# The head of a two-layer attention and gated-MLP kernel: VectorE's order written out, three of four low halves on GpSimd, filling products, two weights loaded earlier

## The chip, the cores and the metric

One Trainium2 chip, one core. The metric is the device time of one execution in microseconds (us); the times stand beside a profiled execution, whose trace gives every instruction's start and length. Engines: PE (TensorE; its weight loads are listed as PEld), DVE (VectorE), ACT (ScalarE), POOL (GpSimd), and SP (SyncE), whose queue issues all DMAs of this kernel.

## What is computed

x has 2048 rows of 640, in float32. Two blocks, A and B, run twice, one after the other (layer 1 is the first A and B, layer 2 the second):

```python
def A(x, wq, wk, wv, wo, beta):        # x is layer-normed; 32 heads of 20; 4 segments of 512 rows
    for s in range(4):
        logits = q[s] @ k[s].T * 20 ** -0.5 + mask      # inside the segment
        a_dot  = softmax(logits) @ v[s]
        a_mem  = (phi(q[s]) @ M) / (phi(q[s]) @ z + 1e-6)
        out[s] = g * a_mem + (1 - g) * a_dot            # g = sigmoid(beta)
        M, z   = M + phi(k[s]).T @ v[s], z + phi(k[s]).sum(0)
    return out @ wo                    # phi(t) = t + 1 if t > 0 else exp(t)
def B(x, w_in, w_sp, b_sp, w_out):     # x is layer-normed
    z1, z2 = split(gelu(x @ w_in), 2)
    return (z1 * (w_sp @ layernorm(z2) + b_sp)) @ w_out
for _ in range(2):
    x = x + A(layernorm(x)); x = x + B(layernorm(x))
```

## The kernel before

Every large product is done in float16 pairs. An operand is scaled by a power of two, its high half is the value cast to float16, its low half what is left over, and a product is three: high by high, high by low, low by high. For a weight that means, on the way in: a DMA brings it in float32 (five tiles of 128 rows, k = 0 to 4); VectorE takes the largest magnitude of each tile (`tensor_reduce`, `largest`); PE turns the 128 partial maxima into a row, VectorE takes their maximum (`pow2_max`, "turn", tiles `wtp`, `wmx`, `wdg`); PE spreads it over the partitions again and VectorE makes the power of two and its inverse (`pow2_spread`, tiles `wbc`, `pw`, `iv`); then for each k ScalarE writes the high half and VectorE the low half (`split_scaled`, lines L90 and L91).

The program is written as a sequence of Python calls. PE's order is exactly the order of these calls (`manual_schedule`). The other engines and the SP queue are put in order by a planner, which picks by priority and by its own estimate of times; `tc.high_priority` raises the priority of what is issued in it, and `tc.issue_after(i)` keeps what is in it behind instruction i. Each engine then works strictly in its order.

`Attention.head` runs once, ahead of layer 1's attention. It loads the first four tiles of x (512 rows, segment 0), w_q and w_k, and later w_v into staging tiles `wstq`, `wstk`, `wstv` (pool `wpro`); normalises x (`xs`), casts the high halves (`hl`, ScalarE), subtracts the low halves (L1277, two on VectorE, two on GpSimd), and transposes both by four DMAs (L1280) into `xt[0]`. Then come w_q, w_k and w_v, each by maxima, scale, split; between them two units of q (`units("q", 0)`, `units("q", 1)`: 15 products of 512 columns each, into the PSUM tile `qp`), two units of k (`kp`), and at the end four tiles of values (`value(t)`, 30 products of 320 columns each, into `vps`, two PSUM buffers). A unit's output casts it to halves (tile `hl`, two buffers shared by q, k and phi(k)), stores these to DRAM (`st`, L1567 and L1568) and for k also makes phi(k) (L1474, L1476, L1485, L1486) and transposes it by DMA (L1493). `start()` writes constant rows into the tiles that q and k are fetched into.

After the head, `run` goes through steps t = -12, ..., -1 (the lead) and 0, 1, 2, ... Each step can hold score products for the row maxima (`mp`, reduced by VectorE in L1641, from t = -8), score products for the softmax (`es`, from t = 0, exponentiated by ScalarE into `P` in L1631, cast in L1649, low half on GpSimd in L1650), products with values (`pv`), and a share of dense products: further units of q and k, value tiles and output projections, in the order "02 03 v4 04 v5 ...". Streams of side work are given times in steps: `fills` (x tiles for later value tiles: L1356 loads, L303 statistics, L318 and L319 halves, L320 transposes), `background`, `weights`, `reads` and `turned`. In layer 1 the stream `weights` brings w_o from t = -11.9 and the second half of w_in (`wi[1]`, "i1") from t = -9.6, as float32 straight into the tiles where their halves will stand (`Weight.inside`: L120 loads, L123 maxima on VectorE, then a split through a staging tile: L139 and L141 on ScalarE, L142 on GpSimd). Those tiles lie in the pools `topi` and `topo`, on the side of SBUF where the head's staging pool `wpro` lay: w_in's tile over the end of `wstk` and over `wstv`, w_o's over the end of `wstq` and over `wstk`. A tile may be written only when those that lay there before are done with.

Of the kernel before, what the change touches and what calls it, by code (L numbers as in the profile page):

```python
# [9 lines left out]
F32 = mybir.dt.float32  # L10
# [24 lines left out]
HP = 2000  # L35
# [18 lines left out]
def pow2_max(g, pool, psum, tag, am, c0, n):  # L54
# [7 lines left out]
    nc.vector.tensor_scalar(dg[:n, :n], g.ident[:n, :n], mx[:n], None, ALU.mult)  # L62
# [31 lines left out]
class Weight:  # L94
# [17 lines left out]
    def inside(self, stage, psum, t0, pace):  # L112
# [22 lines left out]
        def split(k):  # L135
# [4 lines left out]
            for x, a in zip(full, cs):  # L140
# [986 lines left out]
class Attention:  # L1127
# [96 lines left out]
    def head(self):  # L1224
# [3 lines left out]
        with ExitStack() as ctx:  # L1228
            p = ctx.enter_context(tc.tile_pool(name="wpro", bufs=1, side="right", reuse_waits="tile"))
            ctx.enter_context(tc.high_priority(offset=HP))  # L1230
# [6 lines left out]
            st = {nm: p.tile([128, KD, D], F32, name="wst" + nm) for nm in "qkv"}  # L1237

# [4 lines left out]
            def largest(nm, behind):  # L1243
                a = p.tile([128, KD], F32, tag="wamk" + nm, name="wamk")
                with tc.issue_after(behind):
                    for k in range(KD):
                        nc.vector.tensor_reduce(a[:, k:k + 1], st[nm][:, k], AX.X, ALU.max, apply_absolute_value=True)
                i = WNAMES.index(nm)
                return nc.vector.tensor_reduce(g.wam[:, i:i + 1], a, AX.X, ALU.max).ins

            def scale(nm):
                return pow2_scales(g, self.pl1, self.pm, "ms", g.wam, WNAMES.index(nm), 1)

            def split(nm):
                h, l = g.w[nm]
                return [split_scaled(g, h[:, k], l[:, k], st[nm][:, k], WNAMES.index(nm)) for k in range(KD)]

            def units(nm, m, ps):
                for _ in self.unit(0, m, {nm: ps[:, m]}):
                    pass  # L1260
# [15 lines left out]
            for t in (2, 0, 3, 1):  # L1276
                (nc.gpsimd if t > 1 else nc.vector).tensor_tensor(hl[t][:, 1], xs[t], hl[t][:, 0], ALU.subtract)  # L1277
            for t in (0, 1, 2, 3):
# [15 lines left out]
            with tc.issue_after(i[-1]):  # L1294
                attn_scalars(g)
# [695 lines left out]
```

## Time and profile before

| | us |
|---|---|
| median of 3 runs | 2196.34 (2195.93 to 2196.82) |
| the profiled execution's own time | 2197.64 |
| its span, first to last instruction | 2195.9 |
| first q product of the head | at 24.60 |
| first and last product of the head's value tiles | at 53.12 and 71.1 |
| first softmax tile cast (step 0) | at 121.55 |

| stretch (us) | what runs | PE busy | DVE busy | ACT busy | POOL busy | granted clock |
|---|---|---|---|---|---|---|
| 0 to 53.1 | head up to w_v's split | 21.76 | 43.45 | 19.01 | 14.34 | 0.90 |
| 53.1 to 71.3 | value tiles 0 to 3 | 16.82 | 7.35 | 8.45 | 2.81 | 1.00 |
| 71.3 to 121.5 | the lead | 38.66 | 37.05 | 26.57 | 20.40 | 0.90 |

A row of the timeline gives start and length in us, engine, line of the kernel, operation, output<-inputs, partitions x elements and type, and how many like instructions were merged (x5); in square brackets, how long the engine sat idle before it and what ended that. A row of a table by groups gives total busy time, mean ns of one, idle time before them.

### The profile page before, as it was taken

Reading aid. Unit: us, or ns where it says so; the run is one execution under the profiler, and the core shown is the slowest. Engines: PE = TensorE matmul, PEld = TensorE weight load, DVE = VectorE, ACT = ScalarE, POOL = GpSimd, SP = SyncE. Lnnn points to the kernel's source line nnn. Section 1 sums busy time; section 2 is a strip of 40 time slices with the busy share of each in tenths; the row PEclk is TensorE's granted clock in tenths of the full one; section 3 lists DMA queues with packets and bytes.
Section 4 is the critical chain, followed back from the end, with each engine's and each line's share of the span. In section 5 each row is a group of like instructions: output and inputs, shape, how many; then the busy total and the mean of one; then the engine's idle time right before and its main releaser. Section 6 shows DMA issues by size and latency. Waiting matters only on the chain.

```text
span 2195.9 us, 48888 instructions
## 1 busy us (share of the span) xinstructions
PE 2067.9 (94%) x19725; PEld 1250.9 (57%) x19725; DVE 1625.9 (74%) x2951; ACT 1217.8 (55%) x1490; POOL 1086.5 (49%) x704
## 2 busy tenths in 40 slices
PE   4889899999899998999999999999989999999999
PEld 1455565666555554555555556565665555555555
DVE  8678888787777878999745887787776676565464
ACT  3499888787634443323323998888874244322221
POOL 2298988887523442444320987787873233000000
PEclk9999999999999999999999999999999999999999
DMA  5626635457765967888676244344566353978884
GB/s 165 185 68 202 164 87 143 112 135 155 173 193 145 251 176 221 222 224 251 169 231 146 78 123 111 100 124 115 151 172 145 99 156 111 272 199 207 229 205 115
DMA packets 516499, 358.38 MB, mean 163 GB/s; under 512 B 410160, under 2 KB 452720, under 8 KB 511152
## 3 DMA queue, kind: packets, MB, share of 16 engines
q1 hardware_dynamic: 516272, 355.26, 60.6%
q8 instruction: 154, 2.52, 0.5%
q14 instruction: 73, 0.60, 0.1%
HBM read 159.65 MB, written 107.43 MB: 122 GB/s over the span
## 4 chain that ended last, share of the span: by engine, by line
PE 66%; DVE 11%; ACT 8%; DMA 5%; issue 5%; POOL 4%; SPq 1%; ACTq 0%; DVEq 0%; POOLq 0%
PE zp L395 13%; PE cyp L595 4%; PE cyp L870 4%; PE ga L547 3%; PE gb L547 3%; PE yps L1421 3%; PE pv L1684 3%; PE b L799 3%; PE a L799 3%; PE qps L1445 3%; ACT P L1631 3%; PE vps L1389 3%; PE mp L1624 3%; PE kps L1445 2%; POOL PHL L1650 2%
## 5 line engine op out<-in xcount | busy, mean ns | idle before, releaser
L1650 POOL TENSOR_TENSOR PHL<-P,PHL 128x1024 f16<-128x1024 f32 x310 | 659.3, 2135 | 179.8 <-ACT PHL L1649 133.0
L1631 ACT ACTIVATE P<-es,sc 128x1024 f32<-128x1024 f32 x320 | 356.0, 1113 | 89.1 <-PE es L1595 84.7
L1641 DVE TENSOR_REDUCE mx<-mp 128x2 f32<-128x1024 f32 (+2 forms) x384 | 320.9, 861 | 82.6 <-PE mp L1595 79.6
L1649 ACT CAST PHL<-P 128x1024 f16<-128x1024 f32 x320 | 333.4, 1042 | 6.3
L395 PEld LDWEIGHTS <-th 128*128 128x128 f16 x1920 | 187.8, 98 | 167.2 <-issue 6.0
L799 PEld LDWEIGHTS <-wt 128*128 128x128 f16 x1344 | 132.1, 99 | 122.8 <-ACT wt L790 6.0
L1684 PEld LDWEIGHTS <-PHL 128*128 128x128 f16 x5120 | 166.8, 96 | 58.7 <-DVE oat L1705 20.6
L306 POOL TENSOR_TENSOR lnrs<-lnve,mhalf 128x1 f32<-128x1 f32 x78 | 49.7, 644 | 301.0 <-DVE lnve L305 247.3
L547 PEld LDWEIGHTS <-wt 128*128 128x128 f16 x1344 | 131.5, 98 | 112.6
L1684 PE MATMUL pv<-vs,PHL 128*128 128x41 f16 x5120 | 172.6, 181 | 21.3 <-DVE oat L1705 16.9
L395 PE MATMUL zp<-w,th 128*128 128x432 f16 x960 | 180.4, 346 | 5.0 <-ACT z L408 5.0
L395 PE MATMUL zp<-wi,th 128*128 128x432 f16 x960 | 180.4, 346 | 0.2 <-DVE xt L1427 0.2
L1445 PEld LDWEIGHTS <-zb 128*128 128x128 f16 x1200 | 103.0, 99 | 102.8 <-issue 8.5
L784 POOL TENSOR_TENSOR f<-wt 128x1024 f32<-128x1024 f16 x32 | 84.8, 2660 | 127.5 <-DVE wt L793 110.0
L1624 PEld LDWEIGHTS <-qk 64*128 64x128 f16 (+1 forms) x1728 | 65.9, 93 | 129.8 <-issue 98.1
L1624 PE MATMUL mp<-qk 60*128 60x512 f16 (+3 forms) x864 | 107.6, 303 | 18.0 <-DVE mx L1641 12.3
L1421 PE MATMUL yps<-wo,o 128*128 128x320 f16 x720 | 120.4, 304 | 0.0
L1624 PE MATMUL es<-qk 64*128 64x256 f16 (+3 forms) x864 | 105.7, 296 | 12.4 <-ACT P L1631 10.1
L870 PE MATMUL cyp<-w,ut 128*128 128x320 f16 (+1 forms) x630 | 88.1, 299 | 0.0
L1638 DVE TENSOR_REDUCE mx<-mp 128x4 f32<-128x1024 f32 x64 | 77.8, 1215 | 11.0 <-PE mp L1595 10.9
L1389 PE MATMUL vps<-zb,w 128*128 128x320 f16 x480 | 81.1, 299 | 4.1 <-DVE phl L1486 4.1
L1595 PE MATMUL es<-big,maskk 64*128 64x128 f16 (+1 forms) x1280 | 82.4, 206 | 1.5 <-issue 1.5
(318 smaller groups left out, 4166.3 us busy)
## 6 DMA issues: line engine op xcount, KB each, us to landing
wr<-in_B_w_sp_dram SPq DMA_DIRECT2D x32, 1024.0 KB
qk<-st SPq DMA_DIRECT2D x216, 120.0 KB
z<-z SPq DMA_DIRECT2D x32, 432.0 KB
cz<-z SPq DMA_DIRECT2D x32, 432.0 KB
turned<-wt SPq DMA_DIRECT2D x24, 512.0 KB
wt<-turned SPq DMA_DIRECT2D x24, 512.0 KB
st<-qhl SPq DMA_DIRECT2D x40, 256.0 KB
st<-khl SPq DMA_DIRECT2D x40, 256.0 KB
```

Of the source, the lines that this page charges most:

```text
L395: nc.tensor.matmul(zp[:, n, :FHH], a[:, k, :], b[:, k, c:c + FHH], start=(k == 0 and j == 0), stop=(k == KD - 1 and j == 2))
L547: nc.tensor.matmul(o[:, :FHH], wt[:, x, m, :], zb[b][:, y, m, :], start=start and i == j == 0, stop=i == NP - 1 and j == 2, skip_group_che ...
L799: nc.tensor.matmul(o[:, :FHH], w[:, x, m, :], zb[b][:, y, m, :], start=start and i == j == 0, stop=i == NP - 1 and j == 2, skip_group_chec ...
L870: nc.tensor.matmul(yp[n][:, :320], a[:kn[k], k, :], b[:kn[k], k, n * 320:(n + 1) * 320], start=(k == 0 and j == 0), stop=(k == KO - 1 and ...
L1421: nc.tensor.matmul(ps, a[:, k, :], b[:, k, c], start=(i == 0), stop=(i == 14))
L1445: nc.tensor.matmul(ps, a[:, k, c], b[:, k, :], start=(i == 0), stop=(i == 14))
L1624: nc.tensor.matmul(out[:, h, o:o + w], a[r, ac], b[r, bc], start=o == 0, stop=False, skip_group_check=True)
L1631: self.last_of["ACT"] = nc.scalar.activation(self.Pf[t], es, AF.Exp, scale=g.esc).ins
L1641: self.last_of["DVE"] = nc.vector.tensor_reduce(mx[:, e, :, i], mp[:, :, o:o + w], AX.X, ALU.max).ins
L1649: nc.scalar.copy(hl[:, 0], P)
L1650: (nc.gpsimd if t < self.T - self.TAIL or t % 2 == 0 else nc.vector).tensor_tensor(hl[:, 1], P, hl[:, 0], ALU.subtract)
L1684: nc.tensor.matmul(pv[:, i, h, 0:PVC - 1], self.P[u][:, x, h, o:o + 128], v[:, j, h0 + h, :], start=first and h == x == 0 and (u, o, i, j) ...
```

## The change

Five things, all in layer 1's head and lead:

- The low half of x tile 0 is made by VectorE directly behind the four normalisations, those of tiles 1 to 3 by GpSimd; the transposes go in the order 0, 1, 2, 3 as before.
- VectorE's order is written out by `issue_after`: w_q's maxima, its scale with two of w_k's maxima in it, w_q's split whole, the other three of w_k's maxima; then w_k's scale and split with w_v's maxima in the same way. `attn_scalars` (13 small VectorE instructions) go behind w_v's scale. The outputs of the two k units are issued behind w_v's split.
- PE gets filling products (`keep_busy`, 128 x 192, into a PSUM tile `idle` that nobody reads): 100 before w_q's turn, 5 and 16 around its spread, 16 behind w_k's spread, 10 behind w_v's.
- Value tile 0 takes its products in another order, both halves of the columns side by side, with w_v's low half last, and is issued before VectorE's low halves of w_v are done.
- w_in's second half and w_o are loaded from the head, behind the closing of `wpro`, and w_in's maxima are issued behind value tile 1. The lead keeps turn and spread of both, w_o's maxima and both splits, w_in before w_o.

```diff
-    def inside(self, stage, psum, t0, pace):
+    def inside(self, stage, psum):
...
-        by = lambda t, pace, f: [(t + pace * k, lambda k=k: f(k)) for k in range(self.nk)]
-        return (by(t0, pace, load) + by(t0 + 1.7, pace, largest) + by(t0 + 5.9, pace * self.cols / D, split),
-                [(t0 + 4.5, turn), (t0 + 5.5, spread)])
+        return load, largest, turn, spread, split
...
+            idle = self.po.tile([128, 512], F32, tag="pv", name="idle")
...
-            def largest(nm, behind):
+            def largest(nm, ks, behind):
                 with tc.issue_after(behind):
-                    for k in range(KD):
+                    for k in ks:
...
-            def split(nm):
+            def split(nm, behind):
                 h, l = g.w[nm]
-                return [split_scaled(...) for k in range(KD)]
+                with tc.issue_after(behind):
+                    return [split_scaled(...) for k in range(KD)]
+            def keep_busy(n, a):
+                for _ in range(n):
+                    nc.tensor.matmul(idle[:, :192], a[:, :128], a[:, :192], start=True, stop=True)
...
-            for t in (2, 0, 3, 1):
-                (nc.gpsimd if t > 1 else nc.vector).tensor_tensor(hl[t][:, 1], xs[t], hl[t][:, 0], ALU.subtract)
+            with tc.issue_after(i.ins):
+                low = nc.vector.tensor_tensor(hl[0][:, 1], xs[0], hl[0][:, 0], ALU.subtract).ins
+            for t in (1, 2, 3):
+                nc.gpsimd.tensor_tensor(hl[t][:, 1], xs[t], hl[t][:, 0], ALU.subtract)
...
-            largest("q", i.ins)
-            scale("q")
-            i = split("q")
-            largest("k", i[1])
-            units("q", 0, qp)
-            scale("k")
-            units("q", 1, qp)
-            i = split("k")
-            largest("v", i[1])
-            with tc.issue_after(i[-1]):
-                attn_scalars(g)
-            units("k", 0, kp)
-            scale("v")
-            units("k", 1, kp)
-            split("v")
-            for t in range(4):
-                for _ in self.value(t):
-                    pass
-                if t == 0:
-                    with self.hold():
-                        self.start()
+            keep_busy(100, g.mask["q"])
+            largest("q", range(KD), low)
+            dg = turn("q")
+            largest("k", (0,), g.seen)
+            keep_busy(5, g.mask["q"])
+            i = largest("k", (1,), spread("q", dg))
+            keep_busy(16, g.mask["q"])
+            i = split("q", i)
+            largest("k", range(2, KD), i[-1])
+            us = [unit("q", 0, qp), unit("q", 1, qp)]
+            run(us[0])
+            run(us[1], 9)
+            dg = turn("k")
+            largest("v", (0,), g.seen)
+            run(us[1])
+            i = largest("v", (1,), spread("k", dg))
+            keep_busy(16, g.mask["q"])
+            i = split("k", i)
+            i = largest("v", range(2, KD), i[-1])
+            us = [unit("k", 0, kp), unit("k", 1, kp)]
+            run(us[0], 15)
+            run(us[1], 9)
+            with tc.issue_after(i):
+                dg = turn("v")
+            run(us[1], 6)
+            i = spread("v", dg)
+            keep_busy(10, g.mask["q"])
+            with tc.issue_after(i):
+                attn_scalars(g)
+            i = split("v", i)
+            ctx.close()
+            g.top = self.tops()
+            self.ws = self.pool("aws", 3)
+            nc.vector.memset(g.wap, 0.0)
+            self.made = {}
+            for w, pool in ((g.wi[1], g.top[1]), (g.wo, g.top[0])):
+                w.whole(pool)
+                self.made[w.nm] = w.inside(self.ws, self.pm)
+                for k in range(KD):
+                    self.made[w.nm][0](k)
+            values = [self.value(t, t == 0) for t in range(4)]
+            run(values[0], 12)
+            with tc.issue_after(i[-1]):
+                run(values[0])
+                run(us[0])
+                run(us[1])
+                run(values[1])
+                for k in range(KD):
+                    self.made["i1"][1](k)
+                with self.hold():
+                    self.start()
+                for it in values[2:]:
+                    run(it)
...
+    def value(self, t, late=False):
...
+        if late:
+            pairs = [(k, a, wh) for k in range(KD) for a in (xh, xl)] + [(k, xh, wl) for k in range(KD)]
+        todo = [(n, i) for i in range(15) for n in range(2)] if late else [(n, i) for n in range(2) for i in range(15)]
...
-                for w, at, pace in (g.wo, -LEAD + 0.1, 0.45), (g.wi[1], -LEAD + 2.4, 0.5):
-                    w.whole(g.top[w is not g.wo])
-                    work, turns = w.inside(self.ws, self.pm, at, pace)
-                    todo += work
-                    scales.extend(turns)
+                _, _, turn, spread, split = self.made["i1"]
+                scales.extend([(1.6 - LEAD, turn), (2.8 - LEAD, spread)])
+                todo += by(3.4, 0.95, split)
+                _, largest, turn, spread, split = self.made["o"]
+                scales.extend([(5.2 - LEAD, turn), (6.4 - LEAD, spread)])
+                todo += by(2, 0.6, largest) + by(8.3, 0.7, split)
```

`g.seen` is the last VectorE instruction of the last turn (`wdg`). `run(it, n)` draws n pieces from a generator, or all that are left. `run(values[0], 12)` draws all of tile 0, its outputs among them.

More of the change, by code (lines that the diff above doesn't have):

```diff
@@ L1237, in head @@
             st = {nm: p.tile([128, KD, D], F32, name="wst" + nm) for nm in "qkv"}
+            parts = {nm: p.tile([128, KD], F32, tag="wamk" + nm, name="wamk") for nm in "qkv"}
+            idle = self.po.tile([128, 512], F32, tag="pv", name="idle")
             def load(nm):
@@ L1383, in value @@
         yield 450
-        for n in range(2):
-            ps = self.pd.tile([128, L], F32, tag="dn", name="vps")[:, :320]
-            i = 0
-            for k in range(KD):
-                for a, b in ((xh, wh), (xh, wl), (xl, wh)):
-                    nc.tensor.matmul(ps, a[:, k, c], b[:, k, n * 320:(n + 1) * 320], start=(i == 0), stop=(i == 14))
-                    i += 1
-                    if i % 3 == 0:
-                        yield 3 * 136
+        pairs = [(k, a, b) for k in range(KD) for a, b in ((xh, wh), (xh, wl), (xl, wh))]
+        if late:
+            pairs = [(k, a, wh) for k in range(KD) for a in (xh, xl)] + [(k, xh, wl) for k in range(KD)]
+        banks = [self.pd.tile([128, L], F32, tag="dn", name="vps")[:, :320] for _ in range(2)] if late else [None] * 2
+        todo = [(n, i) for i in range(15) for n in range(2)] if late else [(n, i) for n in range(2) for i in range(15)]
+        for n, i in todo:
+            k, a, b = pairs[i]
+            if i == 0 and not late:
+                banks[n] = self.pd.tile([128, L], F32, tag="dn", name="vps")[:, :320]
+            nc.tensor.matmul(banks[n], a[:, k, c], b[:, k, n * 320:(n + 1) * 320], start=(i == 0), stop=(i == 14))
+            if i % 3 == 2:
+                yield 3 * 136
+            if i < 14:
+                continue
+            ps = banks[n]
             def out(ps=ps.rearrange("p (h d) -> p h d", d=DH), v=self.vs[s % 2][:, t % 4, n * 16:(n + 1) * 16, :]):
@@ L1725, in combine, with tops @@
         self.post(2, out)
+    def tops(self):
+        return [self.top.enter_context(self.tc.tile_pool(name=n, bufs=1, side="right", reuse_waits="tile")) for n in ("topi", "topo")][::-1]
     def run(self, nseg=NSEG):
@@ L1856, in turned @@
                 f()
-        if self.stacked < 0:
-            self.head()
         g = self.g
         first = not g.wo.made
-        self.ws = self.pool("aws", 3) if first else None
-        g.top = [self.top.enter_context(g.tc.tile_pool(name=n, bufs=1, side="right", reuse_waits="tile")) for n in ("topi", "topo")][::-1]
+        if first:
+            with g.tc.high_priority(offset=HP):
+                self.head()
+        else:
+            self.ws = None
+            g.top = self.tops()
         streams = [[next(it), i, it] for i, it in zip((0, 1, 1.5, 2, 3, 4), (fills(), background(), weights(), dense(), reads(), turned()))]
```

31 lines of the change are left out of this document (16 added, 15 removed).

## The prediction

> **What bounds the kernel now.** I read the page first, then the table of busy time by stage, then the timeline of the first 130 us, because the whole change lies there.
>
> ```profile
> span 2195.9 us, 48888 instructions
> PE 2067.9 (94%) x19725; PEld 1250.9 (57%) x19725; DVE 1625.9 (74%) x2951; ACT 1217.8 (55%) x1490; POOL 1086.5 (49%) x704
> ...
> PE   4889899999899998999999999999989999999999
> ```
>
> PE is 94% busy over the span, but the first slice of 55 us shows 4 tenths: the head is where PE waits. The stages (columns: length, then busy us of PE, PEld, DVE, ACT, POOL, granted clock, DMA share, GB/s):
>
> ```profile
> 0.00:53.10 53.10, 21.76 (x75) 9.19 (x76) 43.45 (x113) 19.01 (x28) 14.34 (x34) 0.90 0.56 170
> 53.10:71.30 18.20, 16.82 (x122) 11.73 (x121) 7.35 (x17) 8.45 (x16) 2.81 (x3) 1.00 0.72 230
> 71.30:121.50 50.20, 38.66 (x272) 19.78 (x270) 37.05 (x74) 26.57 (x47) 20.40 (x19) 0.90 0.52 141
> 120.00:220.00 100.00, 89.46 (x1404) 55.90 (x1403) 82.20 (x162) 96.83 (x119) 92.73 (x52) 1.00 0.45 142
> ```
>
> The first row is the head up to the first product of values, with VectorE the busiest (43.45 of 53.10). The second is the four value tiles. The third is the lead, 12 steps before the first softmax tile is cast (121.55); PE is idle there for 11.5 us and VectorE is busy for 37.05. In the fourth, ScalarE (96.83) and GpSimd (92.73) set the rate. Nothing there counts from the program's start, so a lead that ends earlier should move all that follows by as much.
>
> **The change, part by part.** *x's low halves and the q scale.* Today VectorE measures four rows of w_q before it makes two of the low halves:
>
> ```profile
> 11.49 2.18 DVE L1274 TENSOR_SCALAR xs<-xs,mvx,rsx 128x640 f32<-128x640 f32 x4 [1.22 <-POOL rsx L1272]
> 14.19 2.75 POOL L1277 TENSOR_TENSOR xhl<-xs,xhl 128x640 f16<-128x640 f32 x2 [2.73 <-ACT xhl L1275]
> 15.61 6.60 SPq L1280 DMA_TRANSPOSE zb<-xhl  x4
> 16.49 1.12 DVE L1277 TENSOR_TENSOR xhl<-xs,xhl 128x640 f16<-128x640 f32 x1
> 18.27 0.81 DVE L1277 TENSOR_TENSOR xhl<-xs,xhl 128x640 f16<-128x640 f32 x1
> 19.08 0.14 DVE L1249 TENSOR_REDUCE wam<-wamk 128x1 f32<-128x5 f32 x1
> 21.84 3.71 ACT L90 ACTIVATE zb<-wstq,iv 128x640 f16<-128x640 f32 x5 [4.54 <-DVE iv L83]
> 24.60 3.38 PE L1445 MATMUL qp<-zb,zb 128*128 128x512 f16 x8 [3.76 <-DMA zb<-xhl]
> ```
>
> After it, VectorE makes one low half directly behind the last normalisation (it ends at 13.67, 11.49 + 2.18) and POOL three, at 2.75/2 = 1.38 each from about 13.4. They end near 14.8, 14.8, 16.2 and 17.6 instead of 19.08 for the last. Four transposes at 6.60/4 = 1.65 then issue until about 21, and land when the first product can start at 22 to 23. VectorE saves one low half (0.8), so the scale and w_q's split come about 1.0 earlier, at 20.8. First q product: about 22.5 instead of 24.60. The 1.12 against 0.81 of the same instruction is the one that ran while POOL's second one (to 16.94) was still running: the two engines slow each other. The Trainium skill, "GPSIMD Engine Reference", section Specifications, says that GpSimd's SBUF interfaces are shared with VectorE when VectorE reads two SBUF inputs; the trace agrees with 0.3 us, and by that rule VectorE's one low half beside POOL's would cost 1.12. That speaks against the move to GpSimd, but for 0.3 us.
>
> *The order of VectorE: w_k and w_v measured before or behind a split, not in its middle.*
>
> ```profile
> 24.30 3.71 DVE L1247 TENSOR_REDUCE wamk<-wstk 128x1 f32<-128x640 f32 x5
> 27.93 2.46 DVE L91 SCALAR_TENSOR_TENSOR zb<-wstq,iv,zb 128x640 f16<-128x640 f32 x3
> 28.86 1.98 PE L1445 MATMUL qp<-zb,zb 128*128 128x512 f16 x7 [0.89 <-DVE zb L91]
> 32.26 3.40 PE L1445 MATMUL qp<-zb,zb 128*128 128x512 f16 x15 [0.32 <-DVE qhl L1469]
> 35.97 3.71 DVE L1247 TENSOR_REDUCE wamk<-wstv 128x1 f32<-128x640 f32 x5
> 39.60 2.46 DVE L91 SCALAR_TENSOR_TENSOR zb<-wstk,iv,zb 128x640 f16<-128x640 f32 x3
> 40.53 2.69 PE L1445 MATMUL kp<-zb,zb 128*128 128x512 f16 x7 [3.15 <-DVE zb L91]
> ```
>
> Five maxima (3.71) stand in the middle of w_q's split and again in w_k's; PE waits 0.89 and 3.15 for the rest. With the split first: w_q's five low halves run 21.7 to 25.9 (0.84 each, from 2.46/3), the q product ends near 26.5 instead of 30.84. Two of w_k's maxima sit in the scale's idle time, the other three end at 28.2. Turn and spread cost what they cost today (19.08 to 21.84, 2.7), with six q products between; plus 0.7 for a q output on VectorE. w_k's split then starts at about 32 and ends at 37.4; today it ends at 39.60 + 2.46 = 42.06. So minus 4.7.
>
> *w_v and the first value tile.*
>
> ```profile
> 41.99 0.14 DVE L241 TENSOR_SCALAR sc<-pw 128x1 f32<-128x1 f32 x1
> 44.50 0.69 DVE L1469 SCALAR_TENSOR_TENSOR khl<-kp,khl 128x512 f16<-128x512 f32 x1 [0.55 <-ACT eq L1468]
> 48.30 4.99 PE L1445 MATMUL kp<-zb,zb 128*128 128x512 f16 x15 [1.70 <-DVE iv L83]
> 49.20 4.07 DVE L91 SCALAR_TENSOR_TENSOR zb<-wstv,iv,zb 128x640 f16<-128x640 f32 x5 [0.90 <-ACT zb L90]
> 53.12 8.31 PE L1389 MATMUL vps<-zb,zb 128*128 128x320 f16 x60
> 55.85 0.49 DVE L1395 SCALAR_TENSOR_TENSOR vs<-vps,vs 128x320 f16<-128x320 f32 x1
> ```
>
> Now the k outputs (four VectorE instructions of 0.69 and a little more) stand between w_v's maximum and its spread; they go behind w_v's split. Mine: three maxima end at 39.7, scale at 43, 13 small scalars (about 0.13 each, 1.7) among five low halves (4.07), end about 48.7 instead of 53.27, minus 4.6. The low-half products of value tile 0 come last in its order, so its 30 products run while the split does, and it ends at 49.2. Today it ends at 53.12 + 30 x 8.31/60 = 57.3. Minus 8.1. Tiles 1 to 3 need 90 x 0.139 = 12.5. VectorE has more to do in that stretch than it does today: eight value outputs (0.49, 3.9 in all), both k outputs (5.9) and w_in's maxima (row below, 5.0), together 14.8 against 12.5. I add 1.3 for PE waiting for a bank: values end at 63.0 instead of 71.3, **minus 8.3**.
>
> *The filling products.* About 150 products of 192 columns go in front of and between the chains, on an idle PE. At the warm rate (0.227 for 512 columns, 3.40/15) one is 0.085 us, so the 16 are 1.4, less than the VectorE and ScalarE work that they cover (scale, then 0.74 + 0.84 for the first split). If cold they are 2.7 and could delay a split's first product by 1.
>
> ```profile
> 40.00:45.00 5.00, 3.05 (x8) 0.73 (x8) 4.42 (x18) 1.17 (x2) 0.00 (x0) 0.63 0.05 17
> 45.00:50.00 5.00, 2.28 (x7) 1.18 (x8) 4.00 (x14) 2.95 (x5) 0.00 (x0) 0.50 0.45 142
> ```
>
> After the 3.15 us gap the clock falls to 0.63 and 0.50, and products of 512 columns take 0.42. Two stretches of some eight products (from 24.60, 3.38 for 8, and from 48.30) cost 8 x 0.2 = 1.6 each, and five cost 1.0 in the lead (row 89.14 below). Between 0 and 3 us of gain over the first two; they hide partly behind VectorE's pace, so I take 0 beyond the times above. The Trainium skill, "TensorE: Matmul & The Clock Gate", section Why this matters for your kernels, puts the loss at idle gaps above about 3 us: the trace agrees (0.89 cost nothing, 3.15 did). By that rule most fillers cover gaps too short to matter, and only the first hundred change anything.
>
> *w_in and w_o earlier.* Ten loads (5 x 320 + 5 x 432 KB, 3.8 MB) leave the lead's start, and five of VectorE's maxima.
>
> ```profile
> 70.36 5.23 SPq L120 DMA_DIRECT2D wi<-in_B_w_in_dram  x1
> 85.97 0.89 DVE L303 BATCH_NORM_STATS2 lnst<-xt 128x6 f32<-128x320 f32 x2 [4.32 <-DMA xt<-in_A_x_dram]
> 88.56 2.00 DVE L123 TENSOR_REDUCE wap<-wi 128x1 f32<-128x864 f32 x2
> 88.70 0.40 PE L1624 MATMUL mp<-qk 60*128 60x384 f16 x4 [4.18 <-DVE mx L1641]
> 89.14 2.32 PE L1445 MATMUL k<-zb,zb 128*128 128x512 f16 x5
> 95.48 0.58 PE L70 MATMUL wbc<-wdg,ones 1*128 1x1 f32 x2 [4.03 <-DVE wdg L62]
> L123 DVE TENSOR_REDUCE wap<-wi 128x1 f32<-128x864 f32 x5 | 5.0, 1037 | 0.0
> wo<-in_A_wo_dram SPq DMA_DIRECT2D x5, 320.0 KB
> wi<-in_B_w_in_dram SPq DMA_DIRECT2D x5, 432.0 KB
> 121.55 1.05 ACT L1649 CAST PHL<-P 128x1024 f16<-128x1024 f32 x1
> ```
>
> Read it as a chain: SP sits 5.23 us in one load, so the x tile for VectorE's statistics comes late; VectorE waits 4.32, the maxima of the scores stand behind it, and PE waits 4.18. Then w_in's maxima (2.00 twice) hold back w_o's scale and PE waits 4.03, after which the clock is half again. With the loads done beforehand I take out most of the 4.18 and 4.03 and some 1.6 of cold clock, and keep the rest, ScalarE's splits of both weights among it, which are only moved within the lead. That is 8 to 10; something comes in their place, above all VectorE (37.05 - 5.0 = 32.05 of work). I take **minus 8**: a lead of 42. Bounds: nothing (the lead keeps 50.2), or PE's own work without its cold clock (38.66 - 1.6 - about 1 = 36), minus 14.
>
> The wait that comes in: w_in's five tiles take the space of w_v's staging tile, so these loads can't start before w_v's split ends (48.7), and on SP the stores of the k outputs, the transposes of phi(k) and the first fetches of q and k may stand behind them. w_o's place is free after w_k's split, and the DMA is nearly idle then (share 0.05 in the row 40 to 45), so w_o may go first. In the stage from 48.7 to 63 the loads are 3.8 MB at the 230 GB/s of the second stage's row, an estimate of 16 us if both wait: just beyond the values' end.
>
> *Sum:* 8.3 + 8 = 16.3 us off 2195.9. The steps after 121.5 I cost at zero; the last of ScalarE's splits stands today right before the first cast, and w_o's will stand there afterwards. The profiled execution took 2197.64 (span 2195.9 and 1.74 around), 1.30 above the median of 2196.34. So 2181.3 for the profiled one, and 2180.0 against the median; I round to **2181** because something new usually waits.
>
> **The rivals.**
> *A, the head gains, the lead does not.* PE would meet a new wait in the lead: the turn of w_in's scale stands at step 1.6, and waits for five maxima that VectorE does only when w_in has landed. For: the 16 us estimate above, and 14.8 us of VectorE work in the value stage. Against: the lead's two largest waits vanish with the loads. Time: 2196.3 - 8.3 = 2188, between 2185 and 2191.5.
> *B, nothing arrives at the end.* ScalarE at 96.83 of 100 sets the steps after the lead; if the splits that now sit in the lead's later half (w_o from step 8.3) push the first softmax tiles, the gain is given back. Against: the work is the same, begun earlier. Time: within 4 us of 2196.3.
> *C, slower: SP.* From 48.7 SP holds the loads; with two buffers for the halves of q, k and phi(k), phi(k) can't be written until the stores of k have landed. ScalarE works in order, so the value outputs behind it wait, and PE with them. One blocked load is 5.23; from three (15.7) on the gain is gone, that is if nearly all ten loads (16) pass ahead of the k stores and the whole of the queue's delay lands on PE, with the lead as long as today. Then 2197 to 2203.
> *D, more than forecast:* the lead at its floor of 36 and values at 61.5: 2196.3 - 9.8 - 14 = 2172.
>
> **How the numbers follow.** Forecast (2176 to 2185) 0.52; A 0.22; D (to 2170) 0.13; B 0.07; C 0.06. The likeliest is 2181. The range goes to D's end and through A: 2171 to 2191, with B, C and a little of either end outside. 0.2% of this kernel is 4.4 us, about what a measurement tells from no change. Faster by more: 0.87; within: 0.07; slower: 0.06.
>
> **What would show it.** Right: the first q product near 22.5, w_k's and w_v's split as five low halves in one run each, the values' end near 63, no wait of over 2 us of PE in the lead for a VectorE maximum, the first cast of a softmax tile near 105, granted clock 1.0 from 20 to 100. Wrong: SP's stores of the k outputs standing after 56; PE waiting at w_in's turn; the first cast near 113 (A); or a cast at 105 and a span that is not 16 shorter (B).

## The result: 13.8 us faster, by a shorter lead more than by the head

| | before | after |
|---|---|---|
| median of 4 runs each, side by side | 2196.14 | 2182.30 (2180.34 to 2183.49) |
| ratio to before, 95% interval | | 0.9941 (0.9925 to 0.9957) |
| the profiled execution, its span | 2197.64, 2195.9 | 2183.49, 2181.8 |
| start of the four normalisations | 11.49 | 10.58 |
| first q product | 24.60 | 22.87 |
| first value product | 53.12 | 46.02 |
| first product of the lead (into `qps`) | 71.28 | 67.34 |
| first softmax tile cast | 121.55 | 108.61 |

The page of the changed kernel, the rows that answer to those of before:

```profile
span 2181.8 us, 49179 instructions
...
PE 2081.9 (95%) x19872; PEld 1263.5 (58%) x19872; DVE 1623.5 (74%) x2950; ACT 1218.4 (56%) x1490; POOL 1089.5 (50%) x705
...
PE   7898999999899998999999999999999999999999
```

PE's first slice went from 4 tenths to 7, though fillers count in it as work. The stages of the changed kernel, cut at the same events as before (columns as before; the last two rows are short stretches used below):

```profile
0.00:46.00 46.00, 31.67 (x222) 21.16 (x223) 36.34 (x101) 14.40 (x22) 17.68 (x35) 1.00 0.65 185
46.00:67.30 21.30, 17.58 (x120) 11.69 (x120) 16.23 (x30) 12.08 (x22) 0.00 (x0) 1.00 0.68 218
67.30:108.60 41.30, 36.76 (x261) 18.93 (x261) 32.42 (x71) 27.98 (x49) 25.09 (x24) 0.96 0.66 166
52.00:60.00 8.00, 7.26 (x52) 4.98 (x52) 7.33 (x11) 4.81 (x9) 0.00 (x0) 1.00 1.01 372
76.00:80.00 4.00, 3.95 (x11) 1.36 (x9) 0.48 (x3) 1.45 (x2) 4.00 (x5) 0.59 0.94 213
```

The stage up to the first value product is 7.1 shorter (53.1 to 46.0), the value stage 3.1 longer (18.2 to 21.3, with VectorE at 16.23 in place of 7.35), the lead 9.0 shorter (50.2 to 41.3): 12.9 at the first cast. The timeline of the changed kernel, its head and lead:

```profile
12.65 4.82 POOL L1286 TENSOR_TENSOR xhl<-xs,xhl 128x640 f16<-128x640 f32 x3 [2.11 <-ACT xhl L1282]
12.68 0.82 DVE L1284 TENSOR_TENSOR xhl<-xs,xhl 128x640 f16<-128x640 f32 x1
...
20.99 4.07 DVE L91 SCALAR_TENSOR_TENSOR zb<-wstq,iv,zb 128x640 f16<-128x640 f32 x5 [0.17 <-ACT zb L90]
22.87 3.40 PE L1494 MATMUL qp<-zb,zb 128*128 128x512 f16 x15 [2.48 <-DMA zb<-xhl]
...
34.04 5.81 DVE L91 SCALAR_TENSOR_TENSOR zb<-wstk,iv,zb 128x640 f16<-128x640 f32 x5 [0.17 <-ACT zb L90]
34.12 6.29 POOL L1220 TENSOR_SCALAR qk<-zb,keep 128x512 f16<-128x512 f16 x5 [16.64 <-ACT zb L90]
46.02 4.94 PE L1435 MATMUL vps<-zb,zb 128*128 128x320 f16 x30 [0.94 <-ACT zb L90]
48.67 1.68 DVE L91 SCALAR_TENSOR_TENSOR zb<-wstv,iv,zb 128x640 f16<-128x640 f32 x2
50.37 2.24 SPq L120 DMA_DIRECT2D wi<-in_B_w_in_dram  x5
52.66 2.50 SPq L120 DMA_DIRECT2D wo<-in_A_wo_dram  x5
55.92 0.38 SPq L1617 DMA_DIRECT2D st<-khl  x1
56.86 8.59 PE L1435 MATMUL vps<-zb,zb 128*128 128x320 f16 x60 [0.56 <-DVE vs L1444]
65.54 0.69 DVE L1518 SCALAR_TENSOR_TENSOR khl<-kp,khl 128x512 f16<-128x512 f32 x1 [3.15 <-ACT eq L1517]
67.34 3.40 PE L1494 MATMUL qps<-zb,zb 128*128 128x512 f16 x15 [1.89 <-DVE vs L1444]
74.54 0.23 PE L1599 MATMUL mup<-vs,pk 128*128 128x147 f16 x1 [2.83 <-DVE wmx L60]
...
108.61 1.04 ACT L1698 CAST PHL<-P 128x1024 f16<-128x1024 f32 x1
```

w_q's split runs whole, before w_k's maxima. w_k's five low halves take 5.81, beside five writes of `start()` on GpSimd. Ten loads stand on SP from 50.37, the store of the first k unit's low half behind them at 55.92. The waits of the changed kernel from 44 to 68 us (total, times, longest) show who hung on that store:

```profile
ACT khl L1514 <- DMA st<-khl: 2.5, 1, 2.5
```

The row of GpSimd's three low halves of x (shortest, median and longest in ns, first and last start) shows that one of them took 2.10 where the others took 1.40; it is the first, which ran beside VectorE's:

```profile
L1286 POOL TENSOR_TENSOR xhl<-xs,xhl x3: 1393/1395/2097, 12.7 to 16.1; 128x640 f16<-128x640 f32 x3
```

### The profile page after: what moved, and what is told of

Same layout as the page of the kernel before. It is cut to its first block, busy times and chain, and to the rows that moved or that the text cites. A ratio compares the mean times of both kernels' runs of the same rounds, so it can differ in the third digit from the quotient of the medians.

```text
span 2181.8 us, 49179 instructions
## 1 busy us (share of the span) xinstructions
PE 2081.9 (95%) x19872; PEld 1263.5 (58%) x19872; DVE 1623.5 (74%) x2950; ACT 1218.4 (56%) x1490; POOL 1089.5 (50%) x705
## 3 DMA queue, kind: packets, MB, share of 16 engines
q1 hardware_dynamic: 516272, 355.26, 60.3%
## 4 chain that ended last, share of the span: by engine, by line
PE 67%; DVE 11%; ACT 8%; DMA 6%; issue 4%; POOL 2%; SPq 1%; ACTq 0%; DVEq 0%; POOLq 0%
PE zp L393 13%; PE cyp L593 4%; PE cyp L868 4%; PE ga L545 3%; PE gb L545 3%; ACT P L1680 3%; PE pv L1733 3%; PE yps L1470 3%; PE vps L1435 3%; PE b L797 3%; PE a L797 3%; PE qps L1494 3%; PE mp L1673 3%; PE kps L1494 2%; ACT PHL L1698 2%
## 5 line engine op out<-in xcount | busy, mean ns | idle before, releaser
L761 ACT ACTIVATE wn<-wr,wiv 128x1024 f16<-128x1024 f32 x32 | 36.6, 1145 | 90.6 <-DVE wiv L749 42.2
L1687 DVE TENSOR_REDUCE mx<-mp 128x4 f32<-128x1024 f32 x64 | 77.8, 1216 | 11.3 <-PE mp L1644 11.2
```

## The experiments

All times are medians of the side by side runs, all ratios to the kernel before. The profiled executions differ by up to 1.5 us before the change has any effect (the normalisations start at 10.0 to 11.5), so small steps are compared from an event inside the head.

| kernel | median, us | ratio and interval | lead starts | first cast | lead |
|---|---|---|---|---|---|
| before again | 2196.72 | 0.9996 (0.9985 to 1.0008) | 69.14 | 120.76 | 51.6 |
| after again | 2180.75 | 0.9934 (0.9921 to 0.9947) | 69.40 | 110.74 | 41.3 |
| new head, old loads | 2191.70 | 0.9977 (0.9966 to 0.9988) | 67.17 | 117.51 | 50.3 |
| old head, early loads | 2190.37 | 0.9973 (0.9961 to 0.9986) | 75.04 | 115.56 | 40.5 |
| no fillers | 2187.54 | 0.9965 (0.9952 to 0.9977) | 69.37 | 111.57 | 42.2 |
| only the first 100 fillers | 2187.63 | 0.9961 (0.9947 to 0.9975) | 69.66 | 114.65 | 45.0 |
| `start()` behind w_v's split | 2180.15 | 0.9931 (0.9917 to 0.9945) | 66.75 | 109.25 | 42.5 |
| w_o loaded before w_in | 2181.27 | 0.9934 (0.9919 to 0.9949) | 65.73 | 106.57 | 40.8 |
| value tile 0 in old order | 2184.37 | 0.9949 (0.9936 to 0.9963) | 68.60 | 110.69 | 42.1 |
| two low halves each | 2183.37 | 0.9954 (0.9936 to 0.9972) | 67.99 | 109.55 | 41.6 |
| three of these together | 2182.70 | 0.9935 (0.9920 to 0.9950) | 64.38 | 104.87 | 40.5 |
| the same, w_in's turn in the head | 2181.82 | 0.9938 (0.9924 to 0.9952) | 63.79 | 106.90 | 43.1 |

**The new head with the loads where they were.**

```diff
-                for k in range(KD):
-                    self.made[w.nm][0](k)
...
-                for k in range(KD):
-                    self.made["i1"][1](k)
...
+                for nm, at, pace, cols in ("o", 0.1, 0.45, D), ("i1", 2.4, 0.5, FH):
+                    load, largest, turn, spread, split = self.made[nm]
+                    todo += by(at, pace, load) + by(at + 1.7, pace, largest) + by(at + 5.9, pace * cols / D, split)
+                    scales.extend([(at + 4.5 - LEAD, turn), (at + 5.5 - LEAD, spread)])
```

> The new head alone: w_in and w_o are loaded, measured and split in the lead at the times of the kernel before. Theory (head and lead give separately, about 4 us at the start of the lead and 9 us in it): without the loads in the value stage the values end a little earlier than in the changed kernel (62 to 65 instead of 65.4), the lead takes about 50 us again, first softmax cast at 113 to 116, span 5 to 8 under the kernel before, about 2188 to 2191. Rival (the head is worth nothing by itself, because the lead waits for its DMAs whenever it begins): cast at 119 or later, span within 3 of the kernel before.

Its timeline, and its table by stage for the lead and for ten microseconds in it:

```profile
67.17 3.40 PE L1490 MATMUL qps<-zb,zb 128*128 128x512 f16 x15
...
117.51 1.05 ACT L1694 CAST PHL<-P 128x1024 f16<-128x1024 f32 x1
```

```profile
67.20:117.50 50.30, 39.61 (x272) 20.17 (x271) 36.63 (x73) 27.21 (x48) 21.71 (x20) 0.86 0.70 173
85.00:95.00 10.00, 5.24 (x18) 1.93 (x18) 7.38 (x19) 1.79 (x3) 1.41 (x2) 0.51 0.75 217
```

The head alone is worth 4.0 at the first cast (3.3 against the second trace of before) and 5.0 in the median (0.0023 of 2196). The cast, at 117.51, misses the expected 113 to 116, because the lead starts later than expected. The lead is as long as before (50.3), with PE idle for half of the ten microseconds from 85 and the clock at 0.51.

**The old head with the loads early** (old order of VectorE, no fillers, low halves two and two, value tiles in the old order; kept are the loads behind w_v's split and w_in's maxima behind value tile 1).

```diff
-            keep_busy(100, g.mask["q"])
-            largest("q", range(KD), low)
...
+            whole("q", i.ins)
+            scale("q")
+            i = split("q", None)
+            whole("k", i[1])
+            run(unit("q", 0, qp))
...
+                if t == 1:
+                    for k in range(KD):
+                        self.made["i1"][1](k)
```

> The early loads alone: the head has the order, the low halves and the outputs of the kernel before and no filling products; w_in and w_o are loaded behind w_v's split and w_in's maxima stand behind value tile 1. Theory: lead of 41 to 43 us instead of 50, values end at 71 to 74 (the loads and maxima stand in the value stage), cast at 113 to 116, span 6 to 9 under the kernel before. Rival (the loads only move the wait, SP and VectorE lose in the value stage what the lead gains): values end at 76 or later, span within 4 of the kernel before.

Its timeline, VectorE's first maximum of w_in, PE at the values and the cast:

```profile
56.77 1.05 DVE L123 TENSOR_REDUCE wap<-wi 128x1 f32<-128x864 f32 x1 [3.40 <-DMA wi<-in_B_w_in_dram]
...
60.70 4.24 PE L1413 MATMUL vps<-zb,zb 128*128 128x320 f16 x30 [2.98 <-DVE vs L1422]
...
75.04 3.40 PE L1472 MATMUL qps<-zb,zb 128*128 128x512 f16 x15 [0.59 <-DVE vs L1422]
...
115.56 1.05 ACT L1676 CAST PHL<-P 128x1024 f16<-128x1024 f32 x1
```

The lead falls to 40.5, so its 9.8 come without the new head, from the early loads and what goes with them: w_in's early maxima and the new times and order of the two scales and splits. Which of these carries it no run separates. But they cost 3.4 in the value stage (18.2 to 21.6), and the lead starts at 75.04, not at 71.28 and not at the expected 71 to 74. PE waits 2.98 there for an output of VectorE, and VectorE stood idle 3.40 before it, at w_in's first maximum, until that tile had landed; no instruction waits for a store in this stage. Together that is 6.0 at the cast and 5.9 in the median (0.0027). Apart the two halves give 10.0 at the cast, together 12.9 (medians: 11 apart, 13.8 together). Counted from the normalisations it is 8.7 apart and 12.0 together, and with the second traces of both kernels 10.1 and 11.3. A reason that fits, though no run isolates it: the same loads lengthen the new head's value stage by 1.5 (19.8 to 21.3) and the old head's by 3.4.

**Without the filling products, and with the first hundred only.**

```diff
             def keep_busy(n, a):
-                for _ in range(n):
-                    nc.tensor.matmul(idle[:, :192], a[:, :128], a[:, :192], start=True, stop=True)
+                pass
```

```diff
-                for _ in range(n):
+                for _ in range(n if n == 100 else 0):
```

> The changed kernel without any filling product. Theory (VectorE's low halves set the pace of the q and k products, so the clock matters little): first q products at 0.43 each until about 26, q unit 0 ends 1 us later, the rest is hidden; span 0 to 2 above the changed kernel. Rival (the fillers carry the gain): clock at half through w_k's and w_v's chains too, first value products cold, span 4 or more above it.

> The changed kernel with the first hundred filling products only. Theory (the gaps between the chains are under 3 us and do not cost the clock): granted clock 1.0 from 20 to 60, span within 1.5 of the changed kernel. Rival (the gaps do cost it): products of 512 columns at 0.43 in the k units or cold value products, span 2 to 4 above it.

The timeline of the one without any, and after it two short stretches of its table by stage (the granted clock is the third number from the end):

```profile
17.61 0.37 PE L58 MATMUL wtp<-ident,wam 128*1 128x128 f32 x1 [14.18 <-DVE wam L1225]
...
21.95 6.15 PE L1492 MATMUL qp<-zb,zb 128*128 128x512 f16 x15 [2.78 <-ACT zb L90]
...
35.66 5.80 DVE L91 SCALAR_TENSOR_TENSOR zb<-wstk,iv,zb 128x640 f16<-128x640 f32 x5 [0.17 <-ACT zb L90]
35.68 0.61 PE L1492 MATMUL kp<-zb,zb 128*128 128x512 f16 x2 [2.35 <-ACT zb L90]
...
37.83 6.02 PE L1492 MATMUL kp<-zb,zb 128*128 128x512 f16 x19 [0.41 <-DVE zb L91]
...
47.64 5.91 PE L1433 MATMUL vps<-zb,zb 128*128 128x320 f16 x30 [1.88 <-ACT zb L90]
```

```profile
38.00:40.00 2.00, 2.00 (x6) 0.47 (x4) 2.00 (x2) 0.51 (x1) 2.00 (x3) 0.50 0.00 0
48.00:50.00 2.00, 2.00 (x10) 1.08 (x9) 2.00 (x5) 2.00 (x4) 0.00 (x0) 0.51 0.00 0
```

Three chains are slow: the first q unit, behind 14.18 of nothing and a few small products (6.15 for 3.40); 19 products of k, which come 2 us behind a wait of 2.35 (0.317 for 0.233 each, clock 0.50 from 38 to 40); and value tile 0 behind a wait of 1.88 (5.91 for 4.94, clock 0.51). For the q unit this is read from its products alone, 0.41 each for 0.227: the clock column still reads 1.00 there.

The three losses do not simply add up. The slow k products cost nothing, since at full speed PE waits 0.41 for each of VectorE's low halves there: from w_k's first low half to the first value product it is 11.98 here (35.66 to 47.64) and 11.98 with the fillers (34.04 to 46.02). Of value tile 0's 1.0 little is left when the lead starts, 21.7 after the first value product here, 21.3 with the hundred and 21.3 in the changed kernel. Counted from the normalisations, the first cast comes 3.0 later than in the first trace of the changed kernel and 1.6 later than in the second, whose q unit was slow too; with the hundred it is 6.4 and 5.0.

The medians with no fillers and with a hundred are equal, 5 to 7 above the changed kernel's two (2182.30, 2180.75); in both the rival came out, and with the hundred by more than its 2 to 4. So the fillers between the chains are worth that, and the hundred alone bring nothing that shows: with them the first q unit still waits 4.12 and takes 6.09. What carries most of that worth stays open: the slow q unit shows in the time of w_k's split, but with the hundred 3.7 stands in the lead (45.0 for 41.3), and without any a part comes only behind the first cast.

**The changed kernel again**, beside the next three.

> The changed kernel itself, beside the three that follow, so that they can be told from it on the same chip. Theory and rival agree: 12 to 16 us under the kernel before, first softmax cast at 108 to 110.

It repeats the lead (41.3) and the result; the cast, expected at 108 to 110, came at 110.74. Its first q unit took 4.93 instead of 3.40 in spite of the fillers. Two other kernels with the same fillers took 5.08 there (the new head with old loads, value tile 0 in the old order) and three took 3.40, so these do not hold the clock there every time. The lead starts at 69.40, no earlier than in the second trace of before (69.14): counted from the normalisations it starts 1.0 earlier, against 3.0 in the first pair of traces.

**`start()` behind w_v's split**, by reading its last low half in GpSimd's first write.

```diff
-            nc.gpsimd.tensor_scalar(t[:, 1], any_, 0.0, g.keep[:, 2:3], ALU.mult, ALU.add)
+            nc.gpsimd.tensor_scalar(t[:, 1], g.w["v"][1][:, KD - 1, :L] if v else any_, 0.0, g.keep[:, 2:3], ALU.mult, ALU.add)
```

> The changed kernel, but GpSimd's five writes of constant rows in start() read w_v's last low half instead of w_k's first high half (both times multiplied by zero), so that they can't run beside w_k's split. Theory (GpSimd slowed VectorE's split of w_k: 5.81 us for five low halves, 1.16 each, instead of 0.84): the five take 4.1 to 4.3, w_v's split ends 1.5 earlier at 48.8, cast 1 to 1.6 earlier, span 1 to 2 under the changed kernel. Rival (the split is paced by something else, ScalarE or the data): five low halves still over 5.5, no gain; or the rows come too late for the first fetches and the lead grows by as much.

Its timeline:

```profile
34.80 4.50 DVE L91 SCALAR_TENSOR_TENSOR zb<-wstk,iv,zb 128x640 f16<-128x640 f32 x5 [0.17 <-ACT zb L90]
...
49.90 3.38 POOL L1220 TENSOR_SCALAR qk<-zb,keep 128x512 f16<-128x512 f16 x5 [13.65 <-DVE zb L91]
```

w_k's five low halves take 4.50 instead of 5.81 (4.1 to 4.3 expected), GpSimd's own five writes 3.38 instead of 6.29: the slowing is shown to come from the two running side by side. Counted from the start of w_k's split, the lead starts 1.3 earlier (32.8 against 34.2 and 34.1) and the first cast 0.1 earlier (75.3 against 75.4): the lead gives it back, where is open, and the median (2180.15 against 2180.75) tells no difference.

**w_o loaded before w_in.**

```diff
-            for w, pool in ((g.wi[1], g.top[1]), (g.wo, g.top[0])):
+            for w, pool in ((g.wo, g.top[0]), (g.wi[1], g.top[1])):
```

> The changed kernel, with w_o's five loads in front of w_in's instead of behind them. Theory (the value stage loses 3 us because the stores of the k outputs stand behind ten loads on SP, and the two buffers of the halves aren't free): w_o's loads go out at about 45, when w_k's staging is free; w_in's at 50 as before; the store of k unit 0 at 53 instead of 55.9; PE's last value product at 63 to 64 instead of 65.4; span 1.5 to 3 under the changed kernel. Rival (the bandwidth of the ten loads is what holds the k stores, or VectorE's work): the values end where they did, span within 1.

Its timeline, SP's queue and PE:

```profile
45.47 2.39 SPq L120 DMA_DIRECT2D wo<-in_A_wo_dram  x5
...
53.28 0.39 SPq L1617 DMA_DIRECT2D st<-khl  x1
65.73 3.40 PE L1494 MATMUL qps<-zb,zb 128*128 128x512 f16 x15 [0.24 <-DVE vs L1444]
```

w_o's loads go out at 45.47, the store stands 2.6 earlier, ScalarE no longer waits for it, and PE's wait ahead of the lead goes from 1.89 to 0.24. From the start of w_k's split the lead starts 2.1 earlier and the cast comes 2.5 earlier. That the store behind the ten loads delays the start of the lead is thus shown; the values themselves, counted so, end only 0.5 earlier, and the median does not move (2181.27 against 2180.75, where 1.5 to 3 less was expected).

**Value tile 0 in the old order**, and **two low halves each**.

```diff
-            values = [self.value(t, t == 0) for t in range(4)]
+            values = [self.value(t) for t in range(4)]
```

```diff
-                low = nc.vector.tensor_tensor(hl[0][:, 1], xs[0], hl[0][:, 0], ALU.subtract).ins
-            for t in (1, 2, 3):
+                for t in (0, 1):
+                    low = nc.vector.tensor_tensor(hl[t][:, 1], xs[t], hl[t][:, 0], ALU.subtract).ins
+            for t in (2, 3):
```

> The changed kernel, with value tile 0 in the old order (the three products of each k together, one half of the columns after the other). Theory: tile 0 is then paced by w_v's low halves and its second half of columns runs behind the split: its end moves from 51.0 to about 52.8, the span 1 to 2 above the changed kernel. Rival (ScalarE and VectorE set the stage after it anyway): no difference within 1.

> The changed kernel, with x's low halves two on VectorE (tiles 0 and 1) and two on GpSimd as in the kernel before, but directly behind the normalisations. Theory (the order matters, GpSimd's third low half does not): low halves end 1.4 earlier than with three on GpSimd, w_q's maxima and scale 0.8 to 1.1 later; the first q product waits for the later of the two, the transposes, and moves by less than 1; span within 1.5 of the changed kernel. Rival (VectorE's time ahead of w_q's maxima is on the path): everything up to the cast 0.8 to 1.1 later.

Neither moves the time by an amount that can be told. In the old order PE follows w_v's low halves one by one, but from the start of w_v's split the lead starts at the same time (21.9 against 22.2 and 22.1) and the cast comes 0.5 later; the median is 3.6 above its neighbour's, with overlapping intervals, and the profile does not show where. With two low halves each, w_q's split begins 9.99 after the start of the normalisations against 9.55 and 9.82, but the first q product comes 12.4 after it against 12.3 and 12.4, and the interval overlaps both of the changed kernel's.

**Three together** (`start()` late, w_o first, 36 fillers for 16 ahead of w_q's split), and the same **with w_in's turn at the end of the head**.

```diff
-            keep_busy(16, g.mask["q"])
+            keep_busy(36, g.mask["q"])
             i = split("q", i)
```

```diff
+                self.made["i1"][2]()
...
-                scales.extend([(1.6 - LEAD, turn), (2.8 - LEAD, spread)])
+                scales.extend([(0.7 - LEAD, spread)])
```

> Three edits to the changed kernel at once: w_o loaded ahead of w_in, GpSimd's constant rows behind w_v's split, and 36 filling products instead of 16 ahead of w_q's split. Theory: 2.1 from the stores of k going out earlier, 1.3 from w_k's split, and 0 to 1.6 from a q unit that is always warm; lead start at 62 to 64, cast at 103.5 to 106; span 3 to 5 under the changed kernel, 2176 to 2179. Rival (the lead is bound by its own DMAs, the fetches of q and k behind the loads, and takes back what comes early): lead of 43 or more, cast at 107 or later, span within 2.

> The kernel e_best0 with w_in's turn at the end of the head and its spread at step 0.7 instead of steps 1.6 and 2.8. Theory (PE's 2.8 us of waiting in the lead come from the turn's PSUM buffer, which VectorE frees only behind the statistics of the next x tiles, and cost the clock besides): no wait of PE over 1.5 between 65 and 80, granted clock 1.0 there, cast 2 to 3 earlier than in e_best0. Rival (VectorE is the bound of the lead's start and the wait only moves to the spread): cast within 1 of it.

The timeline of the second:

```profile
63.79 1.67 PE L1495 MATMUL qps<-zb,zb 128*128 128x512 f16 x7
69.36 3.60 PE L1495 MATMUL qps<-zb,zb 128*128 128x512 f16 x8
...
106.90 1.05 ACT L1699 CAST PHL<-P 128x1024 f16<-128x1024 f32 x1
```

The first has its cast at 104.87, 3.7 ahead of the changed kernel, and a median of 2182.70 where 2176 to 2179 was expected. The second moves PE's wait instead of removing it: the lead's first unit breaks after 7 products and goes on at 69.36, behind the spread, and the cast is 2.0 later than without. Neither beats the changed kernel, so no version here is better than it by an amount that can be told.

**Before again**, for what happens behind the lead.

> The kernel before once more, for the parts behind the head. In the profiles so far layer 1's attention, from the first softmax tile to the last, took 468.4 us in the kernel before and 471.5 and 470.2 in the changed one; layer 2's took 457.9 against 452.9 and 452.2, with the same order of instructions on every engine there. Theory (both are the spread of one execution against another, since nothing of the change is there): layer 1's attention between 468 and 472 and layer 2's between 452 and 457, not 457.9 again; first cast at 120 to 123. Rival (what stands where in time, by the clock or the DMA, makes layer 2's attention of the changed kernel 5 us shorter each time): 457 to 459 again.

Rows of the softmax tiles P in layer 1 and in layer 2 (shortest, median and longest in ns, first start to last end), of the kernel before, of its repetition, of the changed kernel, of its repetition and of the three together:

```profile
L1631 ACT ACTIVATE P<-es,sc x160: 1092/1113/1135, 119.6 to 588.0; 128x1024 f32<-128x1024 f32 x160
L1631 ACT ACTIVATE P<-es,sc x160: 1090/1113/1135, 1199.7 to 1657.6; 128x1024 f32<-128x1024 f32 x160
```

```profile
L1631 ACT ACTIVATE P<-es,sc x160: 1095/1113/1135, 118.8 to 589.2; 128x1024 f32<-128x1024 f32 x160
L1631 ACT ACTIVATE P<-es,sc x160: 1091/1113/1137, 1198.6 to 1656.5; 128x1024 f32<-128x1024 f32 x160
```

```profile
L1680 ACT ACTIVATE P<-es,sc x160: 1091/1114/1137, 107.5 to 579.0; 128x1024 f32<-128x1024 f32 x160
L1680 ACT ACTIVATE P<-es,sc x160: 1094/1114/1137, 1191.6 to 1644.5; 128x1024 f32<-128x1024 f32 x160
```

```profile
L1680 ACT ACTIVATE P<-es,sc x160: 1094/1114/1137, 109.6 to 579.8; 128x1024 f32<-128x1024 f32 x160
L1680 ACT ACTIVATE P<-es,sc x160: 1093/1114/1137, 1189.6 to 1641.8; 128x1024 f32<-128x1024 f32 x160
```

```profile
L1680 ACT ACTIVATE P<-es,sc x160: 1092/1113/1136, 103.7 to 575.1; 128x1024 f32<-128x1024 f32 x160
L1680 ACT ACTIVATE P<-es,sc x160: 1095/1113/1135, 1187.4 to 1642.4; 128x1024 f32<-128x1024 f32 x160
```

Layer 1's attention lasts 468.4 and 470.4 in the two traces of before, 471.5 and 470.2 in the changed kernel's two: no difference that repeats. Layer 2's lasts 457.9 in both traces of before, 452.9 and 452.2 in the changed kernel's two, 455.0 in the three together, and 453.1 to 456.1 in the others. So the expected 452 to 457 did not come and the rival's 457 to 459 did. The program of that part is the same. The longer ones do not follow the first cast.

## Why the prediction was right, and which of its terms were off

The forecast of 2181 stands 1.3 below the measured median, and up to the first cast the mechanism is the one forecast: a head that ends earlier and a lead that loses two waits. Its terms came out like this.

- *x's halves and w_q.* First q product forecast 22.5, measured 22.87 (23.68 in the second trace). VectorE's low half took 0.82 though GpSimd worked beside it from 12.65, where the slowing that I had set against the change would have made it 1.12; GpSimd's took 2.10 there instead of 1.40. The Trainium skill, "GPSIMD Engine Reference", section Specifications, names the shared interface for VectorE's instructions with two SBUF inputs. The trace agrees that the two get in each other's way. That VectorE would pay was my assumption: at this place GpSimd alone did, and in w_k's split both, VectorE 1.3 for five.
- *w_k's split.* Forecast end 37.4, measured 39.85 (34.04 + 5.81). ScalarE's part began 1.2 later than I had it, and the low halves took 1.16 each instead of 0.84. The step that failed is that I looked at VectorE's order alone: `start()` on GpSimd waits only for one instruction of ScalarE, so it ran into the split.
- *The values' end.* Forecast 63.0, that is minus 8.3; measured 67.34, minus 3.9. This is the term that was mis-sized. Tile 0 ended 1.8 late (50.96 for 49.2), inherited from the splits; tiles 1 to 3 took 14.5 for 13.8; and PE waited 1.89 ahead of the lead, for which I had no term. The last is rival C in small: the store behind ten loads holds `khl` of the second k unit (2.5 on ScalarE), VectorE waits 3.15 for it, and the outputs stand behind both; with w_o loaded first PE's wait is 0.24. The old head with early loads lost its 3.4 in another way, nearer to rival A: VectorE's maxima stood ahead of the value outputs, and the first of them waited for w_in. Of the 3.9, about 0.9 is only that this execution reached the normalisations earlier (10.58 for 11.49). My sign for C, stores standing after 56, came true for the second k unit (66.17 and 67.59 on SP) and nearly for the first (55.92); its price of 16 or more did not, since the loads ran at 372 GB/s with the DMA engines full (1.01), not at the 230 that I had taken.
- *The lead.* Forecast 42, minus 8; measured 41.3, minus 9.0, and 40.5 with the old head. Right, and by the loads with what goes with them, as the new head with old loads shows (50.3). The waits of 4.18 and 4.03 are gone. The sign that no VectorE maximum would hold PE for over 2 us failed: w_in's turn holds PE for 2.83, at the place that rival A names, though not for the maxima, which VectorE had finished at 60.3; it comes to the turn late, behind other work. Behind it the clock is 0.59 from 76 to 80, where I had forecast 1.0.
- *The fillers.* Forecast 0, between 0 and 3; measured 5 to 7 in the median, of which 1.6 to 3.0 is found at the first cast. I had priced them from the stretches where the old kernel was cold, and not asked what the new order would be without them: its gaps make three chains slow, though the losses that can be followed there do not add up to the 5. In the prediction I took from the Trainium skill, "TensorE: Matmul & The Clock Gate", section Why this matters for your kernels, that gaps below about 3 us do no harm. Here the clock fell behind shorter ones: value tile 0 took 5.91 for 4.94 behind a wait of 1.88. Another section of the same page, A second HAM failure mode: psum-queue depth-cycling, says that frequent short pauses between groups of products can lower the clock too, and the trace fits that one better (0.50 and 0.51 behind waits of 2.35 and 1.88, with shorter pauses around them). This error and the one at the values' end partly cancel: without fillers the forecast would have been 6.5 too low.
- *Behind the first cast, zero.* Wrong in layer 2, whose attention gave 5.0 in the first pair of traces and 5.7 in the second. Layer 1's took back 3.1 in the first pair and gave 0.2 in the second, so nothing that repeats. The three together show that a head faster by another 3.7 is not sure to arrive: in layer 2 its lead over the changed kernel goes from 4.2 at the first softmax tile to 2.1 at the last, and in the median nothing is left. Rival B's outcome thus holds for those few microseconds; its mechanism, splits that push the first softmax tiles, does not, since these tiles did come earlier. What sets these lengths stays open. Layer 2's engines have the same instructions in the same order in both kernels; how semaphores and waits are laid out can differ between two builds, and no run here isolates that.

So 16.3 forecast against 13.8 measured is minus 8.3 that was minus 3.9, and minus 8 that was minus 9.0, with about 1 behind the lead. In the second pair of traces the lead starts 0.3 later and is 10.3 shorter, and 5.6 of the span's 15.6 come behind the first cast. Counted from the normalisations the two pairs agree: the first cast is 12.0 and 11.3 earlier. The forecast came within 1.3 of the median partly by luck, because layer 2's 5, which I had at zero, stands in for some of what the values' end lacked.

## What to carry to other kernels

Move loads out of a stage that waits for them, but look at what stands behind them on their queue: here the 9.8 that the lead gained cost 3.4 in the value stage of the old head and 1.5 in that of the new one. Look as well at what stands behind an instruction that reads the loaded tile: VectorE's outputs waited behind a maximum whose tile had not landed. When an order is fixed on one engine, check what the others put beside it, and try fillers against the new order's gaps, not against the old trace. A few microseconds won at the start of a long program have to be measured at its end: 3.7 at the first softmax tile were nothing in the median. And trace each kernel twice: the gain from the normalisations to the start of the lead was 3.0 in one pair of traces and 1.0 in the other.

## What the runs showed of the hardware that I had not expected

- The granted clock fell behind gaps shorter than 3 us: 0.51 after a wait of 1.88, 0.50 after one of 2.35 with pauses of 0.3 to 0.4 behind it, 0.59 after one of 2.83. The length of the wait does not decide it: ahead of the first q unit, behind the same 16 fillers, the clock fell to 0.50, 0.50 and 0.55 after waits of 2.11, 2.30 and 2.50, and stayed at 1.00 after 2.13, 2.48, 2.72 and 2.91. What does is open.
- GpSimd and VectorE slow each other by kinds: GpSimd's f16 write by a scalar beside VectorE's split made 0.90 into 1.16 and its own 0.68 into 1.26; of two subtractions side by side, VectorE's took 0.82 here, no more than alone, and GpSimd's 2.10 instead of 1.40; at one place in the kernel before VectorE's took 1.12 and GpSimd's 1.39. What decides who pays is open.
- With ten loads of 320 and 432 KB outstanding, the DMA moved 372 GB/s for 8 us of the value stage, against 230 over the same stage before.
- The same stretch of program took 452.2 to 457.9 in twelve kernels, and came back within 0.7 in the two that were traced twice.
